# Attention with a gated feed-forward block on one core: P times V of the down bank in eight tiles of 64 rows

## The chip, the cores and the metric

One core of a Trainium2 chip runs the whole program. The metric is the device time of one execution in microseconds, lower is better; the kernel before took 2487.45 us (median of three runs, 2485.76 to 2491.65).

## The reference

All arrays are f32. S = 2048 tokens, D = 576, H = 32 heads of 18 columns, a feed-forward width of F = 4608.

```python
xn = layernorm(x)                                  # (2048, 576), eps 1e-5, no weights
q, k, v = split_heads(xn @ wqkv)                   # 32 heads of 18
p  = softmax(q @ k.T / sqrt(18))                   # per head, 2048 x 2048
s  = merge_heads(p @ v) @ wo
g  = silu((gelu_tanh(xn @ w_gate) * (xn @ w_up)) @ w_down)
out = x + s * g
```

The change lies in `p @ v`. The row sums of `p`, by which the softmax is divided, come out of the same matmul: V has a column of ones beside its 18.

## The kernel before

**Precision.** Projections, scores and the feed-forward part are made of pairs of f16 numbers (a high part and a rest); each product is a few f16 matmuls that add up in PSUM. They use 64 of TensorE's rows at a time, two halves of the array side by side with different banks. P times V alone is done in f32, with 128 rows and 32 columns to a matmul.

**Heads go in pairs.** For pair p, `qk1` (line 1458) computes 128 queries by 512 keys of scores for both heads into one PSUM tile, and VectorE takes the row maxima (line 1461). It serves pair p + 1 while `qk2` serves pair p: `qk2` (line 1511) computes the scores the other way round (128 keys by 512 queries, both heads) with the maximum already folded into the matmul, and ScalarE writes their exponentials into a tile P of 128 by 2 by 512 (line 1517). In the main loop `qk1` has one score tile, s1, so the next `qk1` cannot be written before line 1461 has read the last one.

**Bursts.** The P tiles are gathered. `pend` holds pairs of them (the same 128 keys, two blocks of 512 queries), and `burst` multiplies one to four pairs by V at once. For each k tile there are two query blocks b and two heads h, that is four matmuls, one for each 32 partitions of one PSUM bank; over the k tiles of the burst they add up in that bank. Then one VectorE instruction moves the bank into the SBUF tile `osum`, of 128 by 512: a copy for the first burst of a sum (line 1542), an add to what is there for the others (line 1544). `flush` picks the PSUM tag: "md", "ma" or "mb". "md" is two banks; the down projection of the feed-forward part (`DownPair`, line 852) uses both, summed into y by line 872. "ma" and "mb" are one bank each, of the gate and up projections (line 521).

**The order of the work.** It is written down by hand while the program is built, engine by engine. Each step of the main loop issues a `qk2` and a `qk1`, then some matmuls of the feed-forward part, with or without half a `DownPair`; the last step of each cycle is the burst. A planner (`make_plan`, `lost`) chooses how many steps a cycle has and how the other matmuls are spread over them. It reckons with fixed numbers (2.9 us for a burst, and 0.83 us after it until VectorE is free), and none of them is changed.

Of the kernel before, what the change touches and what calls it, by code (L numbers as in the profile page):

```python
# [12 lines left out]
F32 = mybir.dt.float32  # L13
# [3 lines left out]
ALU = mybir.AluOpType  # L17
# [3 lines left out]
P = 128  # L21
# [74 lines left out]
def kernel(ctx: ExitStack, tc: tile.TileContext, x, wqkv, wo, w_gate, w_up, w_down, out):  # L96
    nc = tc.nc
# [1332 lines left out]
    QT, KT, VT, PM = {}, {}, {}, {}  # L1430
# [76 lines left out]
    def qk2(p, qb, kt, tag):  # L1507
        s2 = ps.tile([P, 2, 512], F32, tag=use(tag), name=f"s2_{p}_{qb}_{kt}")
        for h in range(2):
            r = slice(64 * h, 64 * h + 56)  # L1510
            nc.tensor.matmul(  # L1511
                s2[:, h], KT[p][r, P * kt:P * kt + P], QT[p][r, 512 * qb:512 * qb + 512], start=True, stop=True
            )
        pt = ptile(p, f"P_{p}_{qb}_{kt}")
        j0, j1 = set_of(2 * p)[0], set_of(2 * p + 1)[0]
        if j0 == j1:
            nc.scalar.activation(pt, s2, AF.Exp, scale=ETAB[j0])  # L1517
        else:
            nc.scalar.activation(pt[:, 0], s2[:, 0], AF.Exp, scale=ETAB[j0])
            nc.scalar.activation(pt[:, 1], s2[:, 1], AF.Exp, scale=ETAB[j1])  # L1520
        return pt

    final_norm = deque()
    osum = {}

    def burst(todo, tag):

        p, qh, k0, _, _ = todo[0]
        k1 = todo[-1][2]
        t = MTile(tag, [P, 512], F32, 1)  # L1530
        for _, _, kt, pa, pb in todo:
            for b, pt in enumerate((pa, pb)):
                for h in range(2):
                    qd = 64 * b + 32 * h
                    c0 = 38 * kt + 19 * h
                    nc.tensor.matmul(  # L1536
                        t.t[qd:qd + 32, :], VT[p][:, c0:c0 + 32], pt[:, h],
                        start=kt == k0, stop=kt == k1, skip_group_check=True,
                    )
        if k0 == 0:  # L1540
            osum[p, qh] = ap.tile([P, 512], F32, tag="osb", name=f"osb_{p}_{qh}", bufs=2)
            nc.vector.tensor_copy(osum[p, qh], t.t)
        else:
            nc.vector.tensor_tensor(osum[p, qh], t.t, osum[p, qh], op=ALU.add)  # L1544
        t.done()
        if k1 == NT - 1:
            norm(p, qh)
# [115 lines left out]
    while k < 64:  # L1663
# [8 lines left out]
        else:  # L1672
            subtick({"A": 0.9, "V": 0.9, "T": 2.1})
            fill(1.9)
            k0 = k + 1
# [121 lines left out]
    def flush(tags):  # L1797

        for tag in tags:
            if not pend:  # L1800
                return
            n = next((k + 1 for k, u in enumerate(pend) if u[2] == NT - 1), len(pend))
            burst(pend[:n], tag)
            del pend[:n]
# [36 lines left out]
    for p in range(NPAIR):  # L1841
# [3 lines left out]
        for i in range(4 * NT):  # L1845
            s, half = divmod(i, 2)
            qh, kt = divmod(s, NT)
# [5 lines left out]
            if p == NPAIR - 2:  # L1853
                qh = 1 - qh
# [7 lines left out]
            pt = qk2(p, 2 * qh + half, kt, "s2" if more else ("s1", "s2")[i % 2])  # L1862
# [10 lines left out]
            if gs.left == 0 and gs.pair is None and not gs.closed and not plan:  # L1873
# [22 lines left out]
                else:  # L1896
# [8 lines left out]
                    else:  # L1905
                        n = 28 * max(0, len(units) - tail.keep) + (28 if tail.unit is not None else 0)
                        credit = min(credit + min(9, n / (0.75 * (32 - i % 32))), 18)
                        while credit >= 4:
                            u = tail.unit
                            r = 14 if u is None else (u.slots - u.k) or 14  # L1910
                            n = r if r <= 10 or credit >= r else (r + 1) // 2
# [117 lines left out]
```

## Time and profile before

| | |
|---|---|
| median of three runs | 2487.45 us |
| the profiled execution | 2486.80 us, span 2485.0 us |
| granted TensorE clock | 0.999 |
| TensorE matmuls | 2454.2 us busy, 26216 records |
| VectorE | 1832.9 us busy (74%) |
| ScalarE | 1647.7 us busy (66%) |
| GpSimd | 1546.7 us busy (62%) |
| VectorE, maxima of line 1461 | 1252.4 us in 1024 |
| VectorE, line 1544 from md | 93.2 us in 135 |

A busy share counts the time in which at least one instruction of the engine ran. TensorE's matmuls overlap, so their lengths do not add up; what counts for its stream is the distance between starts. An f32 matmul stands in the trace as two records. "PE md_t L852 <- DVE osb L1544" in a table of waits reads: TensorE at line 852 waited for VectorE's line 1544. A time before `<-` in brackets, as in `[0.33 <-PE md_t L1536]`, is how long the engine sat idle ahead of the instruction, with what ended that.

### The profile page before, as it was taken

To read this page: it belongs to the slowest core of one execution; us is meant where nothing else is said; L and a number is where in the kernel's file an instruction comes from. 1 tells how busy PE (TensorE), PEld (TensorE's weight loads), DVE (VectorE), ACT (ScalarE), POOL (GpSimd) and SP (SyncE) were. 2 spreads that over 40 slices of the span, in tenths; PEclk is the share of its full clock that TensorE was granted. 3 is DMA by queue.
4 is the path that set the end of the run, shared out by engine and by line. 5 is a ranking of instruction groups with operands and counts; after the bars stand their busy time and mean duration, and the time that the engine had idled before them with its cause. 6 is when DMAs were issued, how large, how long until landed. Compare 5 with 4: busy or idle time off the path is not lost.

```text
span 2485.0 us, 61455 instructions
## 1 busy us (share of the span) xinstructions
PE 2454.2 (99%) x26216; PEld 1297.8 (52%) x26216; DVE 1832.9 (74%) x2103; ACT 1647.7 (66%) x2002; POOL 1546.7 (62%) x1605
## 2 busy tenths in 40 slices
PE   7999999999999999999999999999999999999998
PEld 6866554444445444445444444444445555544565
DVE  8476677787778787778777777777777777777644
ACT  6222667767676767676766776676766776767774
POOL 4354858667585848484856666567666666577513
PEclk9999999999999999999999999999999999999999
DMA  4633111110211111110202110101111111110124
GB/s 150 162 89 91 41 26 45 25 41 11 61 36 28 44 24 45 25 31 20 59 11 54 16 51 16 54 12 38 31 39 26 43 27 42 25 35 11 42 67 143
DMA packets 135741, 114.01 MB, mean 46 GB/s; under 512 B 65456, under 2 KB 114824, under 8 KB 135468
## 3 DMA queue, kind: packets, MB, share of 16 engines
q1 hardware_dynamic: 132188, 102.15, 16.0%
q0 software_dynamic: 1984, 5.42, 0.7%
q8 instruction: 207, 3.39, 0.6%
q10 hardware_dynamic: 1296, 2.51, 0.3%
q14 instruction: 66, 0.54, 0.1%
HBM read 84.89 MB, written 24.89 MB: 44 GB/s over the span
## 4 chain that ended last, share of the span: by engine, by line
PE 92%; DVE 2%; POOL 2%; DMA 2%; issue 1%; ACT 1%; SPq 0%; ACTq 0%; POOLq 0%; DVEq 0%
PE ma_t L521 19%; PE md_t L852 17%; PE md_t L1536 16%; PE mb_t L521 15%; PE s L1511 9%; PE s L1458 9%; PE ma_t L1536 2%; PE md_t L521 2%; DMA rawa_j<-in_A_wqkv 1%; PE ma_t L1037 1%; PE md_t L1037 1%; PE mb_t L1037 1%; DVE PM L1461 0%; DMA VT<-VS 0%; DVE st L1274 0%
## 5 line engine op out<-in xcount | busy, mean ns | idle before, releaser
L1461 DVE TENSOR_REDUCE PM<-s 128x2 f32<-128x1024 f32 x1024 | 1252.4, 1224 | 345.2 <-PE s L1458 320.4
L1517 ACT ACTIVATE P<-s,etab 128x1024 f32<-128x1024 f32 x960 | 1066.8, 1113 | 568.4 <-PE s L1511 557.8
L521 PE MATMUL mb_t<-XHT,whi_c 64*128 64x512 f16 x1430 | 537.0, 376 | 0.0
L521 PE MATMUL ma_t<-XHT,whi_c 64*128 64x512 f16 x1430 | 537.0, 376 | 0.0
L521 PE MATMUL ma_t<-XHT,wlo_c 64*128 64x512 f16 x1287 | 483.2, 375 | 0.0
L521 PE MATMUL ma_t<-XL,whi_c 64*128 64x512 f16 x1144 | 429.4, 375 | 0.0
L521 PE MATMUL mb_t<-XHT,wlo_c 64*128 64x512 f16 x1144 | 429.4, 375 | 0.0
L521 PE MATMUL mb_t<-XL,whi_c 64*128 64x512 f16 x1144 | 429.4, 375 | 0.0
L1536 PE MATMUL md_t<-P,VT 128*32 128x512 f32 x3680 | 425.6, 596 | 0.0
L1511 PE MATMUL s<-QT,KT 56*128 56x512 f16 x2048 | 396.3, 379 | 0.7 <-ACT P L1517 0.7
L1458 PE MATMUL s<-KT,QT 54*128 54x512 f16 x2048 | 392.4, 377 | 4.6 <-DVE PM L1461 4.4
L521 PEld LDWEIGHTS <-whi_c 64*128 64x128 f16 x5184 | 257.1, 94 | 233.3 <-issue 1.1
L852 PE MATMUL md_t<-dhi_c,hhi 64*128 64x288 f16 x2304 | 331.4, 282 | 0.5 <-DVE osb L1544 0.5
L813 POOL TENSOR_TENSOR hlo<-gv,hhi 128x512 f16<-128x512 f32 x144 | 167.3, 1162 | 263.9 <-ACT hhi L806 216.9
L852 PE MATMUL md_t<-dhi_c,hlo 64*128 64x288 f16 x2304 | 330.9, 282 | 0.0
L852 PE MATMUL md_t<-dlo_c,hhi 64*128 64x288 f16 x2304 | 330.5, 282 | 0.0
L852 PEld LDWEIGHTS <-hhi 64*128 64x128 f16 x4608 | 230.7, 94 | 132.5 <-issue 3.2
L788 POOL TENSOR_SCALAR tw<-tw 128x512 f32<-128x512 f32 x144 | 89.5, 621 | 308.6 <-ACT tw L780 308.5
L1511 PEld LDWEIGHTS <-KT 56*128 56x128 f16 x2048 | 129.5, 93 | 226.5 <-issue 130.3
L872 DVE SCALAR_TENSOR_TENSOR y<-md_t,c_c,y 128x576 f32<-128x576 f32 x272 | 219.7, 808 | 14.0 <-PE md_t L852 13.2
L1536 PEld LDWEIGHTS md_t<-P,VT 128*32 128x32 f32 x3680 | 105.8, 109 | 228.9 <-issue 225.5
L1544 DVE TENSOR_TENSOR osb<-md_t,osb 128x512 f32<-128x512 f32 x135 | 93.2, 690 | 161.6 <-PE md_t L1536 161.3
(256 smaller groups left out, 3870.9 us busy)
## 6 DMA issues: line engine op xcount, KB each, us to landing
draw_c<-in_B_w_down SPq DMA_DIRECT2D x18, 576.0 KB
raw_c<-in_B_w_gate SPq DMA_DIRECT2D x18, 512.0 KB
raw_c<-in_B_w_up SPq DMA_DIRECT2D x18, 512.0 KB
obr<-rd SPq DMA_DIRECT2D x30, 256.0 KB
VS<-vst POOLq DMA_DIRECT2D x16, 304.0 KB, 5.6
VT<-VS SPq DMA_DIRECT2D x16, 304.0 KB
KT<-KD SPq DMA_DIRECT2D x32, 144.0 KB
QT<-QD SPq DMA_DIRECT2D x32, 144.0 KB
```

Of the source, the lines that this page charges most:

```text
L521: m = nc.tensor.matmul(o, lw, xx, start=self.stage == 0 and self.k == 0, stop=self.stage == 1 and self.k == self.slots - 1, skip_group_che ...
L788: gp.tensor_scalar(st["t"], st["t"], 1.0, 1.0, op0=ALU.mult, op1=ALU.add)
L813: gp.tensor_tensor(hs.lo[:, ft], st["v"], hs.hi[:, ft], op=ALU.subtract)
L852: m = nc.tensor.matmul(self.t.t[:, hf, 0:288], a[r, ft, sl], b[r, ft, 288 * hf:288 * hf + 288], start=self.stage == 0 and k == 0, stop=sel ...
L872: nc.vector.scalar_tensor_tensor(yy, y, w.c, yy, op0=ALU.mult, op1=ALU.add)
L1037: m = nc.tensor.matmul(o, a, b, start=self.stage == 0 and self.k == 0, stop=self.stage == 1 and self.k == len(terms) - 1, skip_group_check ...
L1458: nc.tensor.matmul(s1[:, h], QT[p][r, P * qt:P * qt + P], KT[p][r, 512 * kb:512 * kb + 512], start=True, stop=True)
L1461: nc.vector.tensor_reduce(PM[p][:, :, qt, kb:kb + 1], s1, op=ALU.max, axis=AX.X)
L1511: nc.tensor.matmul(s2[:, h], KT[p][r, P * kt:P * kt + P], QT[p][r, 512 * qb:512 * qb + 512], start=True, stop=True)
L1517: nc.scalar.activation(pt, s2, AF.Exp, scale=ETAB[j0])
L1536: nc.tensor.matmul(t.t[qd:qd + 32, :], VT[p][:, c0:c0 + 32], pt[:, h], start=kt == k0, stop=kt == k1, skip_group_check=True,)
L1544: nc.vector.tensor_tensor(osum[p, qh], t.t, osum[p, qh], op=ALU.add)
```

## The change

A burst into "md" takes both banks. Each of its matmuls is cut in two along the 128 keys: keys 0 to 63 add up in the first bank, keys 64 to 127 in the second. So a k tile has eight matmuls of 64 rows and 32 columns. VectorE copies or adds the first bank as before, and then adds the second in an instruction of its own; only then is "md" given back. Bursts into "ma" and "mb" are as they were.

```diff
-        t = MTile(tag, [P, 512], F32, 1)
+        halves = 2 if tag == "md" else 1
+        t = MTile(tag, [P, halves, 512] if halves > 1 else [P, 512], F32, 1)
+        banks_of = [t.t[:, r] for r in range(2)] if halves > 1 else [t.t]
+        n = P // halves
         for _, _, kt, pa, pb in todo:
             for b, pt in enumerate((pa, pb)):
                 for h in range(2):
                     qd = 64 * b + 32 * h
                     c0 = 38 * kt + 19 * h
-                    nc.tensor.matmul(
-                        t.t[qd:qd + 32, :], VT[p][:, c0:c0 + 32], pt[:, h],
-                        start=kt == k0, stop=kt == k1, skip_group_check=True,
-                    )
+                    for r, bank in enumerate(banks_of):
+                        nc.tensor.matmul(
+                            bank[qd:qd + 32, :], VT[p][n * r:n * r + n, c0:c0 + 32], pt[n * r:n * r + n, h],
+                            start=kt == k0, stop=kt == k1, skip_group_check=True,
+                        )
         if k0 == 0:
             osum[p, qh] = ap.tile([P, 512], F32, tag="osb", name=f"osb_{p}_{qh}", bufs=2)
-            nc.vector.tensor_copy(osum[p, qh], t.t)
+            nc.vector.tensor_copy(osum[p, qh], banks_of[0])
         else:
-            nc.vector.tensor_tensor(osum[p, qh], t.t, osum[p, qh], op=ALU.add)
+            nc.vector.tensor_tensor(osum[p, qh], banks_of[0], osum[p, qh], op=ALU.add)
+        for bank in banks_of[1:]:
+            nc.vector.tensor_tensor(osum[p, qh], bank, osum[p, qh], op=ALU.add)
         t.done()
```

VectorE at the first burst into md, before, with what each row waits for (PE and DVE with a number are the semaphores of TensorE and VectorE; PM holds the row maxima, osb is `osum`):

```order
L1461 TENSOR_REDUCE PM_2074<-s_1_15_4369 128x2 [waits PE_49]
L1544 TENSOR_TENSOR osb_0_4169<-md_t,osb_0_4169 128x512 [waits DVE_49,PE_49]
L1461 TENSOR_REDUCE PM_2074<-s_1_16_4404 128x2 [waits PE_49]
L1461 TENSOR_REDUCE PM_2074<-s_1_17_4442 128x2 [waits PE_49]
L870 TENSOR_SCALAR y<-md_t,c_c_3171 128x576 [waits PE_49]
```

The same place with the change:

```order
L1461 TENSOR_REDUCE PM_2074<-s_1_15_4369 128x2 [waits PE_49]
L1548 TENSOR_TENSOR osb_0_4169<-md_t,osb_0_4169 128x512 [waits DVE_49,PE_49]
L1550 TENSOR_TENSOR osb_0_4169<-md_t,osb_0_4169 128x512 [waits DVE_49]
L1461 TENSOR_REDUCE PM_2074<-s_1_16_4421 128x2 [waits PE_49]
L1461 TENSOR_REDUCE PM_2074<-s_1_17_4459 128x2 [waits PE_49]
```

One row is new, L1550; it waits for VectorE's own row before it, and the maxima of the next `qk1` now stand behind it. There are 145 such rows in the program, and no other row is added or moved on VectorE, ScalarE, GpSimd or SyncE.

TensorE at the end of that burst, before (s is a score tile, P an exponential tile, VT the pair's V):

```order
L1536 MATMUL md_t<-P_0_4_4330,VT_3788 32x512 x2
L1536 MATMUL md_t<-P_1_4_4367,VT_3788 32x512 [waits Activation_49]
L1536 MATMUL md_t<-P_1_4_4367,VT_3788 32x512
L1511 LDWEIGHTS KT_1104
L1511 MATMUL s_0_0_5_4399<-QT_1103,KT_1104 128x512 [waits PE_49]
```

With the change:

```order
L1540 MATMUL md_t<-P_0_4_4330,VT_3788 32x512 x4
L1540 MATMUL md_t<-P_1_4_4367,VT_3788 32x512 [waits Activation_49]
L1540 MATMUL md_t<-P_1_4_4367,VT_3788 32x512 x3
L1511 LDWEIGHTS KT_1104
L1511 MATMUL s_0_0_5_4416<-QT_1103,KT_1104 128x512 [waits PE_49]
```

Two matmuls for each tile P have become four; their place among the other rows, and the waits, are the same. Lines below the change are six further down in the new kernel.

## The prediction

> **What bounds the kernel now.** I read the page first, then the table of waits, then the groups by line, then the timeline around the work that the change touches. The page's busy line and the chain of work that ended last:
>
> ```profile
> PE 2454.2 (99%) x26216; PEld 1297.8 (52%) x26216; DVE 1832.9 (74%) x2103; ACT 1647.7 (66%) x2002; POOL 1546.7 (62%) x1605
> PE 92%; DVE 2%; POOL 2%; DMA 2%; issue 1%; ACT 1%; SPq 0%; ACTq 0%; POOLq 0%; DVEq 0%
> ```
>
> TensorE is the bound: it holds 92% of the chain. Next I asked whether it ever waits for VectorE, from the table of its waits:
>
> ```profile
> PE s L1458 <- DVE PM L1461: 4.4, 5, 2.5
> PE md_t L852 <- DVE osb L1544: 0.5, 1, 0.5
> ```
>
> In 1024 QK1 score tiles TensorE waited five times for the row maximum on VectorE (4.4 us), and once for a P times V sum (0.5 us). So VectorE is hidden today; what matters is by how much. Two rules follow: a microsecond added to TensorE's own stream is a microsecond of time, and one added to VectorE is free up to the slack that stands before TensorE's next wait for it.
>
> The groups that the change touches, from the view of line 1536 and that of the tile osb (durations in ns: least, median, most):
>
> ```profile
> L1536 PE MATMUL md_t<-P,VT x3680: 592/592/618, 274.7 to 2443.9; 128*32 128x512 f32 x194
> L1536 PE MATMUL ma_t<-P,VT x416: 590/592/617, 260.7 to 2457.2; 128*32 128x512 f32 x139
> L1544 DVE TENSOR_TENSOR osb<-md_t,osb x135: 678/691/694, 278.4 to 2444.5; 128x512 f32<-128x512 f32 x135
> L1542 DVE COPY osb<-md_t x10: 691/692/692, 414.0 to 2362.5; 128x512 f32<-128x512 f32 x10
> ```
>
> An f32 matmul leaves two records, so 3680 records in md are 1840 matmuls; a k tile (a pair of P tiles) needs four of them, hence 460 k tiles. The 135 + 10 rows on VectorE are 145 bursts into md, 3.2 k tiles each. The 416 records in ma are not changed.
>
> One such burst, and what follows it (timelines of TensorE and of both engines; columns: start, length in us, engine, line):
>
> ```profile
> 1010.47 0.38 PE L1458 MATMUL s<-KT,QT 54*128 54x512 f16 x2
> 1010.77 2.78 PE L1536 MATMUL md_t<-P,VT 128*32 128x512 f32 x24
> ...
> 1012.94 0.61 PE L1536 MATMUL md_t<-P,VT 128*32 128x512 f32 x4
> 1013.49 0.39 PE L1511 MATMUL s<-QT,KT 56*128 56x512 f16 x2
> 1013.62 0.69 DVE L1544 TENSOR_TENSOR osb<-md_t,osb 128x512 f32<-128x512 f32 x1 [0.33 <-PE md_t L1536]
> 1013.72 0.38 PE L1458 MATMUL s<-KT,QT 54*128 54x512 f16 x2
> ...
> 1014.23 1.21 DVE L1461 TENSOR_REDUCE PM<-s 128x2 f32<-128x1024 f32 x1
> ...
> 1014.80 0.29 PE L852 MATMUL md_t<-dhi_c,hhi 64*128 64x288 f16 x2
> ...
> 1015.75 0.38 PE L1458 MATMUL s<-KT,QT 54*128 54x512 f16 x2
> ```
>
> **The change part by part.** *The matmuls.* Records in md go from 3680 to 7360, each with 64 rows. In the burst above 24 records stream from 1010.77 to 1013.37: the last four start at 1012.94, so five passes lie between, 0.43 us each, and a sixth follows. Four column tiles run at once, and a k tile (two passes) costs 0.86 us. Does half the rows mean half the time? These rows say no:
>
> ```profile
> 58.41 0.22 PE L450 MATMUL pv_t<-XHT,wlo_j 128*108 128x128 f16 x1
> ...
> 58.85 0.22 PE L453 MATMUL pv_t<-XHT,wlo_j 128*108 128x128 f16 x1
> 59.01 0.29 PE L698 MATMUL ma_t<-whi_v,XHT 64*128 64x288 f16 x1
> 59.01 0.29 PE L698 MATMUL mb_t<-whi_v,XHT 64*128 64x288 f16 x1
> 59.14 0.28 PE L698 MATMUL ma_t<-wlo_v,XHT 64*128 64x288 f16 x1
> ```
>
> From 58.41 to 58.85 lie eight matmuls of 128 rows and 128 streamed columns, 0.056 us each; one of 64 rows and 288 columns takes 0.13: about 0.44 ns a column both times, whatever the rows. And two 64-row tiles start together (59.01 twice). So I take it that eight tiles stream side by side as four and two do, 0.43 us for a pass of eight: the stream costs what it did. What is added is the start: four records that start one after the other last 0.61 us against 0.592 for one, 0.007 us from tile to tile. Four more tiles put the last one 0.028 us later, once a burst: 145 x 0.028 = 4.1 us. In the Trainium skill, "TensorE: Matmul & The Clock Gate", Part 3, The mechanism, the span of packed tiles is put at one matmul plus about 4 ns per further tile; by that it is an estimated 16 ns a burst, 2.3 us in all. The row is of this very stream, so the sum uses it.
>
> *The pauses at a burst.* A QK1 pair streams 0.22 us from 1010.47, so the burst could start at 1010.69; it starts at 1010.77: 0.08 to 0.09 lost. Its last pass ends at 1013.37 to 1013.39 and QK2 starts at 1013.49: 0.10 to 0.12 lost, about 0.2 us a burst. Rows stay at 64 now, so could this vanish? Two other changes of form bound it: above, 128 to 64 rows at equal columns (0.053 us of streaming after 58.85, then nothing until 59.01: 0.10 lost), and 128 to 64 columns at equal rows:
>
> ```profile
> 31.98 0.33 PE L1311 MATMUL tp<-ident,xn 128*128 128x128 f16 x3
> 32.24 0.25 PE L1313 MATMUL tp<-ident,xn 128*64 128x128 f16 x2
> ```
>
> Three transposes at 0.056 end at 32.15; the next form starts at 32.24, 0.09 lost. A change of the columns alone costs as much as any, and 64 by 128 to 64 by 32 is one. I take no gain, and keep 0.2 x 145 = 29 us as the other end.
>
> *The second add.* 145 more VectorE instructions of 0.69 us. It reads the sum that the first add wrote and waits for it. How a dependent small instruction stands to one that isn't:
>
> ```profile
> 921.69 0.42 DVE L311 TENSOR_REDUCE mg_c<-mb_c 128x2 f32<-128x256 f32 x1
> 922.14 0.17 DVE L321 TENSOR_SCALAR E_c<-mg_c 128x2 int32<-128x2 int32 x1
> 922.22 0.16 DVE L322 TENSOR_SCALAR s_c<-mg_c 128x2 int32<-128x2 int32 x1
> ```
>
> L321 uses L311's result and starts 0.03 after its end; L322 doesn't use L321's and starts 0.09 before its end. So the second add starts 0.03 late and delays the next row by 0.03 + 0.69 = 0.72 us; were it overlapped like an independent one, by 0.61.
>
> What is queued behind it: L1461, the row maximum of the QK1 pair just issued. It starts the moment the first add lets it (1014.23, add's end 1014.31), and ends at 1015.44. The next QK1 (1015.75) writes the same score buffer, so it waits for that end plus the signal. The signal's price, from the two places where TensorE starts as soon as VectorE lets it:
>
> ```profile
> 2052.06 1.22 DVE L1461 TENSOR_REDUCE PM<-s 128x2 f32<-128x1024 f32 x1
> ...
> 2053.33 0.39 PE L1458 MATMUL s<-KT,QT 54*128 54x512 f16 x2
> ...
> 2362.51 0.69 DVE L1542 COPY osb<-md_t 128x512 f32<-128x512 f32 x1 [2.02 <-PE md_t L1536]
> ...
> 2363.26 0.30 PE L852 MATMUL md_t<-dhi_c,hhi 64*128 64x288 f16 x2
> ```
>
> 0.05 and 0.06 us. So the slack is 1015.75 - 1015.44 - 0.06 = 0.25 us, and TensorE is held 0.72 - 0.25 = 0.47 us. The down projection at L852, which needs the md buffer back, stands at 1014.80, 0.49 after the add's end, and would be held 0.72 + 0.06 - 0.49 = 0.29; that hold comes first and is part of the 0.47, not beside it.
>
> I read the same rows at all 145 bursts. 104 lie at 0.47, the first and the last of them:
>
> ```profile
> 278.45 0.69 DVE L1544 TENSOR_TENSOR osb<-md_t,osb 128x512 f32<-128x512 f32 x1 [2.38 <-PE md_t L1536]
> 279.06 1.22 DVE L1461 TENSOR_REDUCE PM<-s 128x2 f32<-128x1024 f32 x1
> 280.58 0.38 PE L1458 MATMUL s<-KT,QT 54*128 54x512 f16 x2
> 281.00 1.23 DVE L1461 TENSOR_REDUCE PM<-s 128x2 f32<-128x1024 f32 x1 [0.73 <-PE s L1458]
> ...
> 2322.11 0.69 DVE L1544 TENSOR_TENSOR osb<-md_t,osb 128x512 f32<-128x512 f32 x1 [1.77 <-PE md_t L1536]
> 2322.72 1.22 DVE L1461 TENSOR_REDUCE PM<-s 128x2 f32<-128x1024 f32 x1
> 2324.24 0.38 PE L1458 MATMUL s<-KT,QT 54*128 54x512 f16 x2
> ```
>
> 19 have less slack (as at 2052.06 and 2362.51 above) and lose 0.57 to 0.73, 13.0 us together. 8 lose 0.15 to 0.30, 2.2 us. 14 lose nothing, mostly where a burst into ma follows, and VectorE waits for that one's end anyway:
>
> ```profile
> 681.98 0.69 DVE L1544 TENSOR_TENSOR osb<-md_t,osb 128x512 f32<-128x512 f32 x1 [0.65 <-PE md_t L1536]
> 683.70 0.69 DVE L1542 COPY osb<-ma_t 128x512 f32<-128x512 f32 x1 [1.02 <-PE ma_t L1536]
> ```
>
> What is late next? After a hold of 0.47 TensorE is 0.47 behind and VectorE 0.72; the 0.25 between them goes into the idle 0.73 before the second maximum (281.00), so the hold doesn't repeat in the burst's cycle. Nor is it won back: TensorE has no idle time to give.
>
> *Sum.* 104 x 0.47 + 13.0 + 2.2 = 64.1, and 4.1 for the starts: 68 us. The profiled execution took 2486.8 us (span 2485.0), 0.65 below the median shown. 2486.8 + 68 = **2555 us**, 2.7% slower. Bounds: with an overlapped second add every hold falls by 0.11, 131 x 0.11 = 14 us less: 2541. If the remaining 0.25 finds no idle time, 131 x 0.72 + 4 = 98: 2585.
>
> **Rivals.** *The pauses vanish* (faster bursts, the add still held): 68 - 29 = +39, 2526 us. For it: the rows no longer change. Against: the transposes' 0.09. 6%. The Trainium skill, "TensorEngine Tiling (Array Packing)", Key Properties, says that a change of tiling mode, not of tile, drains the engine; by that rule this rival gives nothing, and both rows above agree.
>
> *Issue becomes the bound.* A k tile now issues 16 weight loads and 16 matmuls in 0.86 us. The densest run in the trace is one such pair per 0.056 us (58.41 to 58.85), itself paced by its columns. If that is the ceiling, 16 x 0.056 = 0.89: 0.035 x 460 = 16 us more, 2571. 9%.
>
> *Only four tiles run at once.* For it: no row here shows eight. Against: the two halves and the four columns each run together. 0.86 x 460 = 396 more, about 2950. 5%.
>
> *The second add is hidden.* VectorE is 74% busy, and 145 x 0.72 = 104 us fit into its idle time as a share. Against: its place, directly ahead of a maximum with 0.25 of slack. The time would be 2487 to 2492, no change. 3%.
>
> *A shorter burst pays for the add, the other side.* If a 64-row pass streamed in less than 0.43 us: at 3.2 k tiles of two passes a burst, break-even with 68 us is 0.07 us a pass (68 / 145 / 6.4), 17% off. With passes of half the length, 920 x 0.215 = 198 saved: 2486.8 + 68 - 198 = 2357. For it: half the rows are read by each matmul. Against: 0.44 ns a column at 128 and at 64 rows. 4%.
>
> **How the numbers follow.** The forecast has the remaining 73%. The range 2525 to 2590 takes in its bounds, the vanished pauses and the issue bound: 73 + 6 + 9 = 88%, of which I leave 8 for sizes beyond the bounds, so 8 in 10. 0.2%, 5 us, is about what a measurement here can tell from no change. Faster: the short burst, 0.04. Same: the hidden add, 0.03. Slower: the rest, 0.93.
>
> **What would show it.** Right: about 145 waits of QK1 for the maximum, about 0.2 to 0.5 us each (part of a hold shows as L852 waiting for the second add), 60 to 70 us together; the second add 0.03 after the first; passes of eight still 0.43 apart, and a last start 0.05 after the first; the pauses of 0.09 and 0.12 still there. Wrong: passes at another distance than 0.43, pauses gone, or no new wait of TensorE for VectorE.

## The result, and the profile after

The changed kernel takes 2562.08 us (median of 4 runs, 2561.02 to 2565.6), the kernel before 2486.61 in the runs beside it (4 runs, 2484.13 to 2491.65): 1.0301 times the time, interval 1.0288 to 1.0314, or 75.5 us more. The prediction was 2555 us, 68 more, in a range of 2525 to 2590. The profiled execution took 2562.83 us (span 2561.1) at a granted clock of 0.999, so the clock is not in it.

The page of the changed kernel: the busy line, the chain of work that ended last, and three groups (matmuls of the burst, matmuls and weight loads of the down projection).

```profile
PE 2504.0 (98%) x29896; PEld 1377.8 (54%) x29896; DVE 1928.4 (75%) x2248; ACT 1648.7 (64%) x2002; POOL 1547.0 (60%) x1605
PE 83%; DVE 9%; POOL 2%; issue 2%; DMA 2%; ACT 1%; SPq 0%; ACTq 0%; POOLq 0%; DVEq 0%
L1540 PE MATMUL md_t<-P,VT 64*32 64x512 f32 x7360 | 429.0, 593 | 0.0
L852 PE MATMUL md_t<-dhi_c,hhi 64*128 64x288 f16 x2304 | 342.9, 284 | 26.6 <-DVE osb L1550 26.2
L852 PEld LDWEIGHTS <-hhi 64*128 64x128 f16 x4608 | 237.6, 94 | 160.8 <-DVE osb L1550 90.1
```

VectorE has gone from 2% to 9% of the chain, and TensorE from 92 to 83%. VectorE's 145 new instructions and 95.5 us more of busy time are the second adds; ScalarE and GpSimd have as much work as before. TensorE's busy time grew by 50 us although its stream grew by only some 5 (e1 below): matmul ends are modelled, and the drawn length of a matmul runs on into the hold behind it (below).

Two rows of TensorE's waits, and two of those of its weight loads, in the changed kernel (us in total, times, longest):

```profile
PE md_t L852 <- DVE osb L1550: 26.2, 123, 1.1
PE s L1458 <- DVE PM L1461: 2.4, 7, 0.6
```

```profile
PEld L852 <- DVE osb L1550: 90.1, 131, 1.6
PEld L1458 <- issue: 40.0, 128, 0.9
```

One wait of the down projection for a P times V sum has become 123. The other row that has grown is the last, which before read:

```profile
PEld L1458 <- issue: 7.4, 10, 2.7
```

It says "issue" because the records show nothing that it waits for; in 116 of the 128 its place is the second QK1 behind a burst, the one at 1027.98 below. A burst of the changed kernel and what stands behind it, from the timelines of TensorE and VectorE (start, length, engine, line):

```profile
1024.63 0.64 PE L1540 MATMUL md_t<-P,VT 64*32 64x512 f32 x8
1025.20 0.39 PE L1511 MATMUL s<-QT,KT 56*128 56x512 f16 x2
1025.43 0.38 PE L1458 MATMUL s<-KT,QT 54*128 54x512 f16 x2
...
1026.30 0.38 PE L521 MATMUL mb_t<-XHT,whi_c 64*128 64x512 f16 x1
1026.85 0.30 PE L852 MATMUL md_t<-dhi_c,hhi 64*128 64x288 f16 x2 [0.18 <-DVE osb L1550]
...
1027.60 0.38 PE L1511 MATMUL s<-QT,KT 56*128 56x512 f16 x2
1027.98 0.39 PE L1458 MATMUL s<-KT,QT 54*128 54x512 f16 x2
```

```profile
1025.38 0.69 DVE L1548 TENSOR_TENSOR osb<-md_t,osb 128x512 f32<-128x512 f32 x1 [1.84 <-PE md_t L1540]
1026.10 0.69 DVE L1550 TENSOR_TENSOR osb<-md_t,osb 128x512 f32<-128x512 f32 x1
1026.71 1.22 DVE L1461 TENSOR_REDUCE PM<-s 128x2 f32<-128x1024 f32 x1
```

VectorE reads: first add ends at 1026.07, the second starts 0.03 later, and the maximum of the QK1 of 1025.43 ends at 1027.93; the next QK1 starts 0.05 after that. The two QK1 are 2.55 us apart, where they were 2.03 before (1013.72 and 1015.75). The hold of 0.51 or so falls in two pieces. A gate pair streams 0.215 us (the median in the kernel before, from its start to that of L852), so L852 could start at 1026.51 and starts at 1026.85, 0.06 after the second add's end: held 0.34. A QK2 pair streams 0.22, so the QK1 could start at 1027.82 and starts at 1027.98: held 0.16. The table of waits shows 0.18 of the first piece and nothing of the second, since the record of the matmul ahead is drawn with a length of 0.38, of which some 0.16 is not streaming. So a hold is read from starts: over the whole program the starts give some 45 us in front of L852 (about 130 times) and 20 us in front of the QK1 (about 116 times), 68.8 us in all with some small ones. The kernel before has about 1 us of such pauses.

### The profile page after: what moved, and what is told of

It is laid out like the page before. It is cut to its first block, busy times and chain, and to the rows that moved or that the text cites. A ratio compares the mean times of both kernels' runs of the same rounds, so it can differ in the third digit from the quotient of the medians.

```text
span 2561.1 us, 68958 instructions
## 1 busy us (share of the span) xinstructions
PE 2504.0 (98%) x29896; PEld 1377.8 (54%) x29896; DVE 1928.4 (75%) x2248; ACT 1648.7 (64%) x2002; POOL 1547.0 (60%) x1605
## 4 chain that ended last, share of the span: by engine, by line
PE 83%; DVE 9%; POOL 2%; issue 2%; DMA 2%; ACT 1%; SPq 0%; ACTq 0%; POOLq 0%; DVEq 0%
PE md_t L852 17%; PE md_t L1540 16%; PE mb_t L521 16%; PE ma_t L521 13%; PE s L1458 8%; PE s L1511 8%; DVE osb L1550 3%; DVE osb L1548 3%; PE ma_t L1540 2%; PE md_t L521 2%; DVE PM L1461 1%; DMA VS<-vst 1%; PE md_t L1037 1%; PE mb_t L1037 1%; PE ma_t L1037 0%
## 5 line engine op out<-in xcount | busy, mean ns | idle before, releaser
L1517 ACT ACTIVATE P<-s,etab 128x1024 f32<-128x1024 f32 x960 | 1066.8, 1113 | 637.7 <-PE s L1511 629.2
L1540 PE MATMUL md_t<-P,VT 64*32 64x512 f32 x7360 | 429.0, 593 | 0.0
L1458 PE MATMUL s<-KT,QT 54*128 54x512 f16 x2048 | 402.0, 377 | 3.6 <-DVE PM L1461 2.4
L1511 PE MATMUL s<-QT,KT 56*128 56x512 f16 x2048 | 404.5, 379 | 0.7 <-ACT P L1517 0.7
L521 PEld LDWEIGHTS <-whi_c 64*128 64x128 f16 x5184 | 282.0, 94 | 208.7 <-issue 1.1
L852 PE MATMUL md_t<-dhi_c,hhi 64*128 64x288 f16 x2304 | 342.9, 284 | 26.6 <-DVE osb L1550 26.2
L852 PE MATMUL md_t<-dhi_c,hlo 64*128 64x288 f16 x2304 | 341.1, 282 | 0.0
L852 PE MATMUL md_t<-dlo_c,hhi 64*128 64x288 f16 x2304 | 340.7, 282 | 0.0
L852 PEld LDWEIGHTS <-hhi 64*128 64x128 f16 x4608 | 237.6, 94 | 160.8 <-DVE osb L1550 90.1
L1540 PEld LDWEIGHTS md_t<-P,VT 64*32 64x32 f32 x7360 | 124.2, 106 | 214.5 <-issue 211.1
L872 DVE SCALAR_TENSOR_TENSOR y<-md_t,c_c,y 128x576 f32<-128x576 f32 x272 | 219.8, 808 | 14.1 <-PE md_t L852 14.1
```

Of the source, the lines that this page charges most:

```text
L521: m = nc.tensor.matmul(o, lw, xx, start=self.stage == 0 and self.k == 0, stop=self.stage == 1 and self.k == self.slots - 1, skip_group_che ...
L852: m = nc.tensor.matmul(self.t.t[:, hf, 0:288], a[r, ft, sl], b[r, ft, 288 * hf:288 * hf + 288], start=self.stage == 0 and k == 0, stop=sel ...
L872: nc.vector.scalar_tensor_tensor(yy, y, w.c, yy, op0=ALU.mult, op1=ALU.add)
L1458: nc.tensor.matmul(s1[:, h], QT[p][r, P * qt:P * qt + P], KT[p][r, 512 * kb:512 * kb + 512], start=True, stop=True)
L1511: nc.tensor.matmul(s2[:, h], KT[p][r, P * kt:P * kt + P], QT[p][r, 512 * qb:512 * qb + 512], start=True, stop=True)
L1540: nc.tensor.matmul(bank[qd:qd + 32, :], VT[p][n * r:n * r + n, c0:c0 + 32], pt[n * r:n * r + n, h], start=kt == k0, stop=kt == k1, skip_gr ...
```

## The experiments

My theory: the time comes from the second add alone, by way of the maximum behind it on VectorE and a slack of 0.25 us, and the eight-tile stream costs its later start only. The rivals: eight tiles that cost more than four (issue, or the stream), and a wait that depends on the split itself rather than on the add. All times are medians; the ratio is against the kernel before on the same chip. Distances are medians over 110 to 130 typical bursts, from starts in the trace.

**e1_no_second_add: the split without its sum.** (The copy is written as an add of a tiny number, an instruction of the same size.)

```diff
-            nc.vector.tensor_copy(osum[p, qh], banks_of[0])
+            nc.vector.tensor_scalar(osum[p, qh], banks_of[0], 1e-30, None, op0=ALU.add)
...
-        for bank in banks_of[1:]:
-            nc.vector.tensor_tensor(osum[p, qh], bank, osum[p, qh], op=ALU.add)
```

> The changed kernel without the VectorE instruction that adds the second bank: keys 64 to 127 of each k tile of the down bank are left out of the sums (and the first copy adds 1e-30, so that no row sum is zero). My theory (the cost is the second add, queued ahead of the row maximum): what is left are the later starts of tiles five to eight, 0.023 to 0.027 us a burst, 145 times 0.025 = 4 us over the kernel before, about 2490 us; the 0.036 us by which the first add now starts later after the last matmul lies inside the slack of 0.25 us. Rival (the eight tiles themselves, their 7360 matmuls and weight loads, carry half of the loss or more): 2525 us or more.

Measured: 2491.83 us against 2487.19, 1.0019 (1.0010 to 1.0028), 4.6 us more. So all 7360 records of 64 rows and 32 columns cost about 5 us beside the 3680 of 128 rows, and the other 71 us go with the second add. A burst of it (both engines):

```profile
1011.72 2.81 PE L1540 MATMUL md_t<-P,VT 64*32 64x512 f32 x48
...
1014.46 0.39 PE L1511 MATMUL s<-QT,KT 56*128 56x512 f16 x2
1014.63 0.69 DVE L1548 TENSOR_TENSOR osb<-md_t,osb 128x512 f32<-128x512 f32 x1 [0.39 <-PE md_t L1540]
1014.69 0.38 PE L1458 MATMUL s<-KT,QT 54*128 54x512 f16 x2
...
1015.24 1.21 DVE L1461 TENSOR_REDUCE PM<-s 128x2 f32<-128x1024 f32 x1
...
1016.73 0.38 PE L1458 MATMUL s<-KT,QT 54*128 54x512 f16 x2
```

48 records last 2.81 us, where 24 of the kernel before lasted 2.78. The maximum of the QK1 of 1014.69 ends at 1016.45 and the next QK1 starts 0.28 later: the slack is there, and the QK1 are 2.04 apart, as before.

**e2_add_alone, e3_add_16_columns, e4_add_256_columns: an add of chosen size, without the split.** The kernel before, with a second add from the same bank behind the first, of 512, 16 or 256 columns. The edit of e2; in e3 the two `512` are 16, in e4 256.

```diff
+        if tag == "md":
+            o = osum[p, qh][:, 0:512]
+            nc.vector.tensor_tensor(o, t.t[:, 0:512], o, op=ALU.add)
         t.done()
```

> The kernel before (four tiles of 128 rows, one bank), with a second VectorE add of 128 by 512 from the same bank after each burst into md, so that the sums of these bursts count twice. My theory: the maximum comes 0.72 us later against a slack of 0.25, a hold of 0.47 us in 104 bursts and 15 us in the others: 64 us more, about 2551 us. The rival (eight tiles): less than 38 us more, below 2525.

> As with the add alone, but the second add has 16 columns, about 0.18 us and 0.03 for its wait, 0.21 us together (the sums of these columns count twice). My theory: this is inside the slack of 0.25 us, so 104 bursts lose nothing, and only the 19 with less slack lose 0.1 to 0.2 us each: 3 us more, 0 to 5. Rival (every VectorE instruction that stands in this place costs its length): 145 times 0.21 = 30 us more.

> As with the add alone, but with 256 columns, about 0.43 us and 0.03 for its wait, 0.46 us together (the sums of these columns count twice). My theory, a slack of 0.25 us and then every hundredth counts: 104 times 0.21 = 22, 19 times about 0.4 = 8, 30 us more, 25 to 36. Rivals: in proportion to the full add, 64 times 0.46 / 0.72 = 41 us; by its length, 145 times 0.46 = 67 us.

Measured, with the distance from the first add's end to the maximum (-0.08 in the kernel before) and that from QK1 to QK1 (2.039 before):

| second add | to the maximum | its delay | QK1 to QK1 | time | ratio | more |
|---|---|---|---|---|---|---|
| 16 columns | 0.125 us | 0.21 us | 2.039 us | 2491.39 us | 1.0016 (1.0007 to 1.0025) | 4.2 us |
| 256 columns | 0.376 us | 0.46 us | 2.243 us | 2518.49 us | 1.0123 (1.0109 to 1.0137) | 31.3 us |
| 512 columns | 0.64 us | 0.72 us | 2.510 us | 2553.62 us | 1.0262 (1.0248 to 1.0276) | 66.4 us |

A delay of 0.21 is nearly free, one of 0.46 holds TensorE by 0.204, one of 0.72 by 0.471: each time the delay less 0.25. This is the slack that the prediction read as 1015.75 - 1015.44 - 0.06, measured by what it lets through. For 256 columns the rivals stood at 41 and 67 us. The burst of the 512-column case (both engines):

```profile
1020.10 0.69 DVE L1544 TENSOR_TENSOR osb<-md_t,osb 128x512 f32<-128x512 f32 x1 [1.78 <-PE md_t L1536]
1020.19 0.38 PE L1458 MATMUL s<-KT,QT 54*128 54x512 f16 x2
...
1020.83 0.69 DVE L1547 TENSOR_TENSOR osb<-md_t,osb 128x512 f32<-128x512 f32 x1
...
1021.07 0.38 PE L521 MATMUL mb_t<-XHT,whi_c 64*128 64x512 f16 x1
1021.43 1.22 DVE L1461 TENSOR_REDUCE PM<-s 128x2 f32<-128x1024 f32 x1
1021.58 0.30 PE L852 MATMUL md_t<-dhi_c,hhi 64*128 64x288 f16 x2
...
1022.70 0.39 PE L1458 MATMUL s<-KT,QT 54*128 54x512 f16 x2
```

Its waits of TensorE at L852, and those of the weight loads there, make a trap:

```profile
PE md_t L852 <- DVE osb L1547: 7.4, 15, 1.2
```

```profile
PEld L852 <- DVE osb L1547: 87.3, 134, 1.7
```

At the matmuls only 15 waits and 7.4 us, with 66.4 us lost. L852 is held by about 0.30 here (1021.58, where a gate pair's 0.215 us after 1021.07 allows 1021.28), but shows no idle time in front of it. With the split it is held by 0.34 and shows 0.18. The weight loads' row does name the wait, 134 times, but its 87.3 us are more than was lost in all; by the distances of starts the holds at L852 make about 45. Idle time in these tables tells where a wait is, and not how long.

**e5_replanned and e6_before_replanned: tell the planner.** The planner reckons with 0.83 us after a burst until VectorE is free. e5 gives it the two adds that the change needs; e6 gives the kernel before the same number, as the control.

```diff
     def lost(steps, exp):
-        vec = 0.83
+        vec = 1.59
```

> The changed kernel, with the planner told that VectorE is free 1.59 us after a burst in place of 0.83 (0.66 + 0.036 from the last start to the first add, less 0.52 to QK2, plus two adds). The plan then puts one more pair of gate and up matmuls, 0.216 us, ahead of the down projection in the step after a burst, in 121 of 137 steps. My theory: the hold per burst falls from 0.51 to 0.30 us, 26 us less than the changed kernel: about 2536 us, 2525 to 2545. The rival (the eight tiles): no change, 2562 us.

> The kernel before, with the planner's same number at 1.59. My theory: TensorE is never held after a burst there, so the new plan has nothing to win: 2487 us, within 10 us. Were it as much faster as the replanned changed kernel is against the changed one, then the plan in itself would be better and the holds would not be the reason.

Measured: e5 takes 2529.36 us, 1.0174 (1.0146 to 1.0202) of the 2488.78 before (one of its four runs took 2536.9, the others 2529.2 to 2529.5); e6 2485.58, 0.9992 (0.9982 to 1.0001), no difference, though its two QK1 behind a burst are 2.254 us apart instead of 2.039, so the plan did change. Going by the ratios, e5 has 32 us less than the changed kernel. In its plan one more gate pair (0.216 us of matmul work) stands between the burst and L852, and the distance from QK1 to QK1 is unchanged at 2.550: work has moved into the hold. What is left in front of L852 is 15.2 us in 113 pauses, and 19.2 us in 104 in front of the QK1. The place of the first, in TensorE's timeline of e5:

```profile
1014.22 0.38 PE L521 MATMUL mb_t<-XL,whi_c 64*128 64x512 f16 x1
1014.55 0.30 PE L852 MATMUL md_t<-dhi_c,hhi 64*128 64x288 f16 x2
```

0.33 us from start to start for 0.215 of streaming, a hold of 0.12, where the changed kernel had 0.34.

**e7_rows_reversed: the other half of the keys first.** The same eight matmuls with keys 64 to 127 ahead of 0 to 63.

```diff
-                    for r, bank in enumerate(banks_of):
+                    for r, bank in list(enumerate(banks_of))[::-1]:
```

> The changed kernel with the two halves of the rows issued in the other order: keys 64 to 127 first, so that the last matmul of a burst is one of rows 0 to 63. My theory has no use for the order: 2562 us, within 4 us, with a burst and a hold as they were. If the 0.036 us by which VectorE's first add now starts later after the last matmul come from the last tile's rows being the lower half, that distance goes back from 0.696 to 0.660 us, and the time falls by up to 5 us.

Measured: 2564.53 us, 1.0303 (1.0279 to 1.0326), the same as the changed kernel. It was to tell where a surprise came from: in the changed kernel, e1 and e5 the first add starts 0.696 us after the start of the last matmul, in those without the split 0.660. With the halves in the other order it is still 0.696, so it isn't due to which half ends last.

**e8_second_bank_act_pool and e9_act_copy_no_pool_add: take the second bank off VectorE.** In e8 ScalarE copies the second bank to SBUF and GpSimd adds it; e9 leaves GpSimd's add out, and writes the first copy as e1 does. The edit of e8:

```diff
         for bank in banks_of[1:]:
-            nc.vector.tensor_tensor(osum[p, qh], bank, osum[p, qh], op=ALU.add)
+            half = stage.s.tile([P, 512], F32, tag="half", name=f"half_{p}_{qh}_{k0}", bufs=1)
+            nc.scalar.activation(half, bank, AF.Copy)
+            nc.gpsimd.tensor_tensor(osum[p, qh], half, osum[p, qh], op=ALU.add)
```

> The changed kernel with the second bank copied to SBUF by ScalarE and added to the sum by GpSimd; VectorE keeps the first add alone. My theory: the maximum is again 0.08 us ahead of the first add's end, and md comes back when ScalarE's copy ends, about when the first add does; ScalarE has 0.6 us idle ahead of the exponential there, so its 0.69 us cost at most 0.1 to 0.2 a burst: 2490 to 2515 us. The rival (the eight tiles): 2525 us or more, since the matmuls are those of the changed kernel. A miss on the upper side for another reason: GpSimd's add of about 1.2 us, 145 times, delays the gate's own work there.

> The kernel with the second bank on ScalarE and GpSimd, without GpSimd's add: the second bank is copied to SBUF and goes nowhere, so keys 64 to 127 of each k tile of the down bank are left out of the sums (the first copy adds 1e-30). It tells apart what made that kernel slow. If it is ScalarE's copy, which there starts only when VectorE's first add has ended (0.69 us after it starts, in its queue ahead of the exponential), the time stays at 2575 to 2590 us. If it is GpSimd's 145 adds of 1.27 us, in the way of the gate's work, the time falls by 20 us or more, to 2540 to 2570, where the late return of md, about as late as in the changed kernel, still costs some 40 us or more.

Measured: e8 takes 2590.34 us, 1.0408 (1.0388 to 1.0427), the slowest of all, where I expected 2490 to 2515. e9 takes 2567.90, 1.0321 (1.0304 to 1.0339), so GpSimd's adds are some 22 us of it and the split with the copy on ScalarE 80. Part of the 22 shows at the burst: in most bursts of e8 VectorE's first add has a second wait, for GpSimd's last sum, and the medians are 0.765 us from the last matmul's start to that add (0.696 in e9) and 2.670 from QK1 to QK1 (2.603 in e9). The rest was not followed up. One row of ScalarE's waits and a burst of e8 on VectorE, ScalarE and TensorE:

```profile
ACT half L1551 <- DVE osb L1548: 180.3, 125, 2.6
```

```profile
282.61 0.69 DVE L1548 TENSOR_TENSOR osb<-md_t,osb 128x512 f32<-128x512 f32 x1 [2.44 <-PE md_t L1540]
...
283.33 0.60 ACT L1551 ACTIVATE half<-md_t 128x512 f32<-128x512 f32 x1 [1.37 <-DVE osb L1548]
283.82 1.11 ACT L1517 ACTIVATE P<-s,etab 128x1024 f32<-128x1024 f32 x1
283.98 0.30 PE L852 MATMUL md_t<-dhi_c,hhi 64*128 64x288 f16 x2
...
284.59 0.30 PE L852 MATMUL md_t<-dhi_c,hlo 64*128 64x288 f16 x2
284.98 0.39 PE L1511 MATMUL s<-QT,KT 56*128 56x512 f16 x2
```

The copy starts 0.03 us after VectorE's first add ends. I had reckoned that the two banks would be read side by side; the program as built has ScalarE wait for VectorE's counter before it reads the other bank of the same tile:

```
L1551 ACTIVATE half_0_1_4415<-md_t 128x512 [waits DVE_49]
```

So md comes back nearly as late as with two adds (L852 at 283.98, 0.05 after the copy and 0.68 after the first add's end, which is 0.78 with two adds), and behind the waiting copy stands the exponential of the next QK2 (L1517), which ends at 284.93. The QK2 after it writes the score tile that this exponential reads, and starts at 284.98 instead of 284.71 (0.12 after the last L852). Its pauses over the program: about 47 us in some 130 places in front of L852 and 31 to 33 in some 120 in front of the QK2. The wait has only moved to an engine whose next instruction TensorE waits for too. Whether reading the banks side by side would pay was not tried.

**e10_replanned_further: the planner told 1.90.** As e5, with 1.90 us; most steps after a burst then hold eleven gate and up pairs and no down projection.

> The changed kernel with the planner's number at 1.90. The plan now puts 11 pairs of gate and up matmuls and no down projection into most steps after a burst: 2.8 us between the two QK1 where 2.55 are needed. My theory: the hold is gone in these steps, and what is left over the kernel before is the later starts and what the other steps lose by being shorter: 2490 to 2515 us. The rival (the eight tiles): no less than the 2529 us that the first new plan gave.

Measured: 2547.91 us, 1.0241 (1.0226 to 1.0257), worse than e5, where I expected 2490 to 2515. Behind the burst all is well: the QK1 are 2.814 us apart with as much work between them, and pauses there are 2.8 us in 10 and 2.0 us in 8. But TensorE waits elsewhere; the costliest of its new waits in e10, then one such place (both engines):

```profile
PE md_t L852 <- DVE y L872: 23.1, 103, 0.3
```

```profile
296.69 0.28 PE L852 MATMUL md_t<-dhi_c,hhi 64*128 64x288 f16 x2
...
296.89 1.23 DVE L1461 TENSOR_REDUCE PM<-s 128x2 f32<-128x1024 f32 x1 [0.60 <-PE s L1458]
...
298.03 0.81 DVE L870 TENSOR_SCALAR y<-md_t,c_c 128x576 f32<-128x576 f32 x1
...
298.29 0.38 PE L1458 MATMUL s<-KT,QT 54*128 54x512 f16 x2
...
298.89 0.30 PE L852 MATMUL md_t<-dhi_c,hhi 64*128 64x288 f16 x2 [0.22 <-DVE y L870]
```

The down projection driven out of the step behind the burst now stands in neighbouring steps, close upon the one before it. md is given back by VectorE's L870 or L872, which stands behind a maximum (to 298.12) and ends at 298.84. L852 could start at 298.51, 0.22 after the QK1, and starts at 298.89. Behind L870 or L872 such pauses make about 43 us in 114 places. A plan needs room behind a burst and between two uses of md at once.

No version beat the kernel before.

## Why the prediction was right, step by step

**TensorE is the bound, and VectorE counts from its slack on.** Right. Delays of 0.21, 0.46 and 0.72 us gave 4.2, 31.3 and 66.4 us.

**The stream is unchanged; eight tiles run side by side.** Right. Passes of eight are 0.429 us apart, against 0.43. The last burst above has eight starts in 0.64 us where one record has 0.589: 0.05 / 7 = 0.007 us a tile, the predicted step. First to last start grew from 2.190 to 2.217 us, 0.027 for a forecast of 0.028, and e1 measured 4.6 us (2.5 to 7.0) for a forecast of 4.1. The estimate of 16 ns a burst by the Trainium skill, "TensorE: Matmul & The Clock Gate", Part 3, The mechanism (about 4 ns a further tile), is too low for this stream.

**The pauses at a burst stay.** Right. From the QK1 to the first P times V start 0.306 us in both kernels, from the last one to the QK2 0.525 and 0.521. The gain of up to 29 us isn't there.

**The second add starts 0.03 us after the first, delays the maximum by 0.72, and the slack is 0.25.** Right, all three: 1026.10 after 1026.07; -0.083 to +0.642 is 0.725; 0.25 from e2 to e4. The signal from VectorE to TensorE took 0.053.

**The hold of 0.47 in a typical burst.** This is the term that was mis-sized: it measured 0.51 (QK1 to QK1 2.552 instead of 2.039). The working took the first add to start where it did, and only the second to come late. But the first add itself starts 0.036 us later behind the last split matmul (0.696 instead of 0.660). 0.036 + 0.72 - 0.25 = 0.51. Burst by burst, up to the second QK1 or the next burst, the starts give 104 bursts held by 0.50 to 0.55 us, 19 by 0.60 to 1.0 and 22 by less than 0.1; the prediction had 104 at 0.47, 19 at 0.57 to 0.73, and 8 small ones and 14 at nothing. In e2, where there is no split, the hold was 0.471, just as worked out, and 64.1 forecast stood against 66.4 measured (61.7 to 68.6 by the interval). In e1 the 0.036 is there and costs nothing, being inside the slack. It counts only when the second add has used the slack up, in the bursts that are held: 0.036 x 123 is about 4.4 us (from QK1 to QK1 2.552 with the split and 2.510 without it, a step of 0.04). Then 4.6 (e1) + 66.4 (e2) + 4.4 = 75.4, for 75.5 measured. The sum was 68; the other 3 us of difference lie within what e1 and e2 leave uncertain.

**Where the hold shows.** 0.29 at L852 as a part of 0.47 became 0.34 of 0.51, again by the 0.036. The sign that the prediction named, about 145 waits of QK1 for the maximum, did not come: the tables name L852 131 times at its weight loads, and QK1 for the maximum only 7 times. The distances of starts show both pieces; of the second the tables show only the "issue" row of the QK1's weight loads. The larger piece, 0.34 of the 0.51, lies at L852.

**The hold doesn't repeat and isn't won back.** Right: the pauses stand in the step behind each burst. They make 68.8 us, and the later last starts 0.027 x 145 = 3.9; the other 3 us of the 75.5 were not traced to a place.

**The rivals.** Issue as the bound and four tiles at once would both be seen in e1: 16 and 396 us more against 4.6 measured. Pauses that vanish would make e1 faster by about 25, and a shorter burst by 190: neither. The hidden add is excluded by e2.

## What to carry to other kernels

An engine that is busy 74% of the time has no slack to give by its share: what an added instruction costs is its delay to the next instruction that the bounding engine waits for, less the slack that stands there, times the number of places. Cutting the contraction of a matmul in two gave no stream time here, and bought a second sum on another engine. A planner's fixed number that stands for the old tail is part of such a change: it was worth 32 of 75 us, and overshooting it lost about 17 of them again, with new waits at the next buffer that was not ready.

## What the runs showed that was not expected

- **The first reader comes 0.036 us later behind eight tiles than behind four.** From the start of the last matmul to the start of VectorE's first add 0.696 instead of 0.660 us, with the second add and without it, and with either half first. The QK2 behind the same matmul is not later (0.521, 0.525), so the delay lies on the way to the other engine and not in TensorE's stream. In both kernels a burst's last matmul signals; of the others 6 in all do in the kernel before, and none with the split. The Trainium skill, "TensorE: Matmul & The Clock Gate", Part 3, The cost: per-tile semaphore tail, says that the tail after packed tiles grows with their number, by 4.7 ns a tile, and by 26.3 ns for each tile that signals. By that, four more tiles are an estimated 19 ns, so the direction agrees and the size does not. No run varied the number of tiles or signals otherwise, and the cause stays open.
- **Eight f32 tiles of 64 by 32 fill the array like four of 128 by 32.** 0.429 us a pass both times, 2.81 for 48 records against 2.78 for 24.
- **A hold of 0.3 us can be missing from the matmuls' waits**, as in e2: of about 45 us of holds at L852 the matmuls' row shows 7.4, and the weight loads' row 87.3.
